# Sigmoid attention and SwiGLU on one core: one eviction moved ahead of the Silu, side work dealt evenly, and the output stage's banks and loads in another order

## The chip, the cores and the metric

The kernel runs on one core of a Trainium2 chip. The metric is device time in microseconds (us), from the first to the last instruction of one execution with what lies around it. Five engines work from queues of their own, each in the order in which its instructions were written: TensorE (PE, matmuls; its weight loads are PEld), VectorE (DVE), ScalarE (ACT), GpSimd (POOL, all but unused here) and SyncE (SP), which issues the DMA transfers.

## The reference, cut to what matters

```python
scores = q @ k.T / 8 - log(448)            # 4 batches, 12 heads, 448 tokens, head dim 64
x = (sigmoid(scores) @ v)                  # -> 1792 tokens x 768
xn = x / sqrt(mean(x * x) + 1e-6) * rms_g
g, val = xn @ w_gate, xn @ w_val           # 768 -> 1536
out = (silu(g) * val) @ w_out              # 1536 -> 768, float32
```

## The kernel before, in words

Every float32 product is made of float16 products: an operand is split into a rounded part ("hi", made by ScalarE) and the rest ("lo", made by VectorE), and three of the four cross products are added up in PSUM (`PARTS`). The weights arrive as 64-bit words and are turned into float32 by three VectorE steps (L430, L431, L432). On top of that both matrix stages of the SwiGLU use a seven-product scheme in place of eight block products, so sums and differences of operands are formed first and the products of several blocks share partial sums.

There are three stages. **Attention** (to about 137 us) computes scores, sigmoid and the product with v, and normalises. The **quads** (137 to 447 us) compute `silu(g) * val`: one quad is one 256-wide chunk `fc` of d_ff (12 of them) for one half `n` of the batches, 24 quads in all. A quad is seven products of nine 448-column matmuls each (1.70 us a product). The result goes to a DRAM scratch tensor `y_d`. The **output stage** (447 us to the end) multiplies by `w_out`, for seven pairs `p` of token tiles, with products of eighteen 384-column matmuls each.

The order within a quad (`quad`, L529) is written by hand. The first product goes into bank `cb`; ScalarE copies it to `y[:, 0]` (L534). A second product is added to the same bank (L540 copies it to `y[:, 1]`), so it has to wait for the copy L534. A third product goes into `cd`. Then `m2` makes product `ca`, VectorE adds `y[:, 0]` into `g_b` (L551) and ScalarE takes its Silu (L552). `m7` adds another product to `cb`, and ScalarE copies that to `c_b` (L556): the copy of the chained tile. All quads but two leave four closures, `c22`, `m4`, `m3` and `ends`, in a list `behind`; the next quad runs them one by one between its own products. `m4` adds a last product to the old quad's `cb` bank, so it may start only when L556 has read that bank; `m4` comes right after the next quad's first product. `ends` writes the quad's result to `y_d`.

At five places of each quad `fill(0)` to `fill(4)` put side work into the VectorE and ScalarE queues: the split of the next chunk's weights (`split_w`), and three of the 48 steps that prepare `w_out` (`split_o`: load a 768 KB chunk, L430, L431, L432, and for each pair of chunks a rounding L616 on ScalarE and a difference L619 on VectorE). `DONE` says which share of the quad's parts has been issued after each fill. In the last two quads, (11, 0) and (11, 1), the fills load and split the first halves of the activations instead (`load_a`, `split_a`, L646 and L647), through three landing buffers `fa`.

In the output stage seven PSUM banks `pss[p]` take first the "even" and then the "odd" product of each pair. Four of them are tiles of their own (`o`), the others are halves of two-bank tiles (`o2`). ScalarE evicts after the even product (L1007) and after the odd one (L757, `out_end`). VectorE's work stands in one list, `line`, which `run_line` deals out by a small clock of costs: four 2304-column sums of `w_out` (L635, each with a ScalarE rounding L628), seven odd splits, four differences `los` (L631), then `split_p(0)`, `split_p(1)` and so on (adds L662, roundings L665, differences L669). `pair_rest(p)` then makes five products per pair.

Of the kernel before, what the change touches and what calls it, by code (L numbers as in the profile page):

```python
# [24 lines left out]
def attention_then_swiglu(  # L25
# [24 lines left out]
    P = 128  # L50
# [6 lines left out]
    NFC = DFF // P  # L57
# [20 lines left out]
    N_NORM = 34  # L78
    LEFT = {(0, 0): (26, 26, 24, 20, 16), (1, 0): (15, 14, 10, 9, 5), (0, 1): (4, 1, 0, 0, 0)}
    EARLIER = {(0, 0): (2, 0, 0, 0, 0), (1, 0): (0, 0, 0, 0, 0), (0, 1): (0, 0, 1, 1, 1)}  # L80
    DONE = (0.15, 0.3, 0.6, 0.9, 1.0)

    bias_s = const.tile([P, 1], F32, name="bias_s")
    ones = const.tile([P, P], F32, name="ones")
# [5 lines left out]
    XW = 7 * NK * S  # L90
    FW = 7 * NK * P
    RW = 2 * DM
    HW = 2 * S
    SL = NK * S
    xc_room = const.tile([P, NQ * XW], F32, name="xc")
    w_room = const.tile([P, 2 * RW + 3 * FW], F32, name="wr")
# [6 lines left out]
    def words(of, at, *shape, dt=F32):  # L103
        n = math.prod(shape) if dt != F16 else math.prod(shape) // 2
        t = of[:, at : at + n]
        if dt != F32:
            t = t.bitcast(dt)
        names = " ".join("abcdef"[: len(shape)])
        sizes = dict(zip("abcdef", shape))
        return t.rearrange(f"p ({names}) -> p {names}", **sizes)  # L110
# [38 lines left out]
    NM = NFC // 2  # L149
    NT = NQ * NTOK  # L150
    NP = NT // 2
# [8 lines left out]
    TW = NM * P  # L160
    a_o = [words(w_room, n * TW, 2, NM, P, dt=F16) for n in range(NP)]
    assert NP * TW <= 2 * RW + FW
    fa = [words(w_room, 2 * RW + FW + n * TW, NM, P) for n in range(3)]
    F_AT = (xc_room, 4 * OW), (room, C_WORDS + 3 * OW)
    f_o = [words(of, a, 5, NM, P) for of, a in F_AT]
    hs_o = [words(of, a + 5 * TW, 2, 5, NM, P, dt=F16) for of, a in F_AT]
# [5 lines left out]
    def bank(name):  # L172
        return ps_m.tile([P, 512], F32, tag="m", name=name)

    def banks(name):
        return ps_s.tile([P, 2, 512], F32, tag="sc", name=name)
# [275 lines left out]
    def run_load():  # L452
        if loads:
            loads.pop(0)[1]()
# [54 lines left out]
    def run_behind():  # L509
        if behind:  # L510
            behind.pop(0)()

    def product(ps, fc, n, a, b, more=False):

        w = win[fc % 2]
        for c in range(NK):
            for m, (l, r) in enumerate(PARTS):
                nc.tensor.matmul(  # L518
                    ps,
                    w[:, l, b, c],  # L520
                    xc[n, a][:, r, c],
                    start=(not more and c == 0 and m == 0),
                    stop=(c == NK - 1 and m == 2),
                    skip_group_check=more,
                )
# [3 lines left out]
    def quad(fc, n, fill, whole=False):  # L529
        y = y_b[len(y_of) % 3]  # L530
        y_of.append((fc, n))
        pb = bank("cb")
        product(pb[:, :S], fc, n, 0, 0)
        nc.scalar.activation(y[:, 0], pb[:, :S], AF.Copy)  # L534
        run_behind()
        fill(0)
        run_behind()

        product(pb[:, :S], fc, n, 4, 5, True)
        nc.scalar.activation(y[:, 1], pb[:, :S], AF.Copy)  # L540
        run_behind()
        fill(1)
        pd = banks("cd")[:, 0]
        product(pd[:, :S], fc, n, 5, 2)
        run_behind()
        fill(2)

        def m2():
            pa = bank("ca")
            product(pa[:, :S], fc, n, 1, 1)  # L550
            tt(g_b, pa[:, :S], y[:, 0], ALU.add)  # L551
            nc.scalar.activation(g_b, g_b, AF.Silu, scale=UNIT)  # L552

        def m7():
            product(pb[:, :S], fc, n, 3, 4, True)
            nc.scalar.activation(c_b, pb[:, :S], AF.Copy)  # L556

        def c22():
            tt(c_b, pd[:, :S], c_b, ALU.add)

        def m4():
            product(pb[:, :S], fc, n, 6, 3, True)
            stt(y[:, 0], pb[:, :S], SH * UNIT, g_b, ALU.mult, ALU.mult)

        def m3():
            product(pd[:, :S], fc, n, 2, 6, True)
            tt(y[:, 1], pd[:, :S], y[:, 1], ALU.add)  # L567
            nc.scalar.activation(y[:, 1], y[:, 1], AF.Silu, scale=UNIT)  # L568

        def ends():  # L570
            stt(y[:, 1], c_b, SH * UNIT, y[:, 1], ALU.mult, ALU.mult)
            i, m = fc % 2, fc // 2
            nc.sync.dma_start(
                y_d[n * NTOK : n * NTOK + NTOK, :, i, m].rearrange("t p x -> p t x"),
                y.rearrange("p j s -> p (j s)").rearrange("p (t x) -> p t x", x=P),
            )

        if whole:
            m7()
            c22()  # L580
            m2()
            fill(3)
            m4()
            m3()
            fill(4)
            behind.extend((wait, wait, ends))
        else:
            m2()
            fill(3)
            m7()  # L590
            fill(4)
            behind.extend((c22, m4, m3, ends))

# [2 lines left out]
    def load_o(c):  # L596
        nc.sync.dma_start(raw_o.rearrange("p f w -> p (f w)"), w_out[c * P : c * P + P, :])
# [42 lines left out]
    def load_a(p, i):  # L640
        nc.sync.dma_start(fa[(p + i * NP) % 3], y_d[2 * p, :, i])

    def split_a(p, i):
        f = fa[(p + i * NP) % 3]
        return [
            lambda: nc.scalar.activation(a_o[p][:, 0], f, AF.Copy),  # L646
            lambda: tt(a_o[p][:, 1], f, a_o[p][:, 0], ALU.subtract),  # L647
        ]
# [31 lines left out]
    line, done, ready = [], set(), set()  # L680
# [110 lines left out]
    def at_once(parts):  # L791
        return [x for x in parts if x[0] is not wait]
# [50 lines left out]
    with tc.manual_schedule():  # L843
# [59 lines left out]
        def fill_norm(where):  # L903
            left = LEFT[where]

            def fill(at):
                run_load()
                while len(later) > left[at]:
                    later.pop(0)[0]()
                for part, *_ in third[: EARLIER[where][at]]:  # L910
                    part()
                del third[: EARLIER[where][at]]

            return fill
# [3 lines left out]
        def fill_steps(*steps):  # L918
            def fill(at):
                for p in steps[at]:  # L920
                    if p == fed[0]:
                        load_a(p, 0)
                        fed[0] += 1
                    else:
                        for part in split_a(p, 0):
                            part()

            return fill

        def fill_with(parts):  # L930
            parts = at_once(parts)
            n = len(parts)

            def fill(at):
                run_load()
                run_load()
                while len(parts) > n - round(n * DONE[at]):
                    parts.pop(0)[0]()

            return fill  # L940
# [4 lines left out]
        for fc, n in order:  # L945
            if (fc, n) in LEFT:
                fill = fill_norm((fc, n))
            elif (fc, n) == (1, 1):
                fill = fill_with(third)
            elif fc + 1 < NFC:  # L950
                if n == 0:
                    split[fc + 1] = split_w(fc + 1)
                parts = at_once(split[fc + 1][n])
                if (fc, n) == (2, 0):
                    outs = split_o()
                    load_o(0)
                    share = -(-len(outs) // (2 * (NFC - 3)))
                new, outs = outs[:share], outs[share:]
                k = len(parts) // max(len(new), 1)
                for i, x in enumerate(new):  # L960
                    parts.insert((i + 1) * k + i, (x, 0.0))
                fill = fill_with(parts)
            elif n == 0:
                assert not outs
                fill = fill_steps([], [0, 1, 2], [], [0, 3], [1, 2, 4, 5])
            else:
                fill = fill_steps([3, 6], [4], [5], [6], [])
            quad(fc, n, fill, (fc, n) in ((1, 1), (NFC - 1, NQ - 1)))


# [2 lines left out]
        pss = [bank("o") for _ in range(4)]  # L973
        for _ in range(2):
            both = banks("o2")
            pss += [both[:, 0], both[:, 1]]
        pss = [pss[x] for x in (0, 1, 3, 4, 5, 2, 6)]
        for p in range(3):
            load_a(p, 1)
        load_p(0)  # L980
# [1 line left out]
        def odd(p):  # L982
            hi, lo = split_a(p, 1)

            def both():
                hi()
                lo()
                if p + 3 < NP:
                    load_a(p + 3, 1)

            return [(None, 0.0, {("even", p)}), (both, 0.95, [("odd", p)])]

        sums, los = sums_o()
        line.extend((x, cost, ()) for x, cost in sums)
        for p in range(NP):
            line.extend(odd(p))
        line.extend((x, cost, ["w"]) for x, cost in los)
        line.append((lambda: load_p(1), 0.0, ()))
        for p in range(NP):
            if p > 1:  # L1000
# [43 lines left out]
```

## Time and profile before

| | |
|---|---|
| median of 3 timed runs | 619.41 us (616.53 to 622.06) |
| the profiled execution | 611.99 us, span 610.2 us |
| TensorE busy, VectorE, ScalarE | 571.0 us (94%), 438.6 (72%), 264.8 (43%) |
| mean granted TensorE clock | 0.985 of full speed |
| TensorE busy from 200 to 440 us (240 us) | 221.5 us |
| TensorE busy from 440 to 500 us (60 us) | 48.9 us |
| TensorE busy from 500 to 560 us (60 us) | 60.0 us |

A row of the timeline gives the start, the length, the engine, the line and operation, the output and inputs, how many instructions were merged, and in brackets how long the engine had been idle and which instruction ended that. A row on waits gives the waiting engine and line, the instruction that it waited for, and the total, the number and the longest. The clock row has one digit for each fortieth of the span (15.3 us).

### The profile page before, as it was taken

Reading aid. Unit: us, or ns where it says so; the run is one execution under the profiler, and the core shown is the slowest. Engines: PE = TensorE matmul, PEld = TensorE weight load, DVE = VectorE, ACT = ScalarE, POOL = GpSimd, SP = SyncE. Lnnn points to the kernel's source line nnn. Section 1 sums busy time; section 2 is a strip of 40 time slices with the busy share of each in tenths; the row PEclk is TensorE's granted clock in tenths of the full one; section 3 lists DMA queues with packets and bytes.
Section 4 is the critical chain, followed back from the end, with each engine's and each line's share of the span. In section 5 each row is a group of like instructions: output and inputs, shape, how many; then the busy total and the mean of one; then the engine's idle time right before and its main releaser. Section 6 shows DMA issues by size and latency. Waiting matters only on the chain.

```text
span 610.2 us, 10226 instructions
## 1 busy us (share of the span) xinstructions
PE 571.0 (94%) x4230; PEld 307.4 (50%) x4230; DVE 438.6 (72%) x576; ACT 264.8 (43%) x397; POOL 0.7 (0%) x6
## 2 busy tenths in 40 slices
PE   8999999999999989898898989899997969999997
PEld 6546554445544544354454445445553536666664
DVE  4697999988769667586876767674584882777761
ACT  5888898875423323323233332423456250222220
POOL 0000000000000000000000000000000000000000
PEclk9999999999999999899999999999997979999999
DMA  8999999830154652727365273612654175155411
GB/s 265 250 221 249 275 273 220 167 61 1 31 152 138 191 136 83 185 74 191 102 180 153 82 186 91 155 32 56 186 178 167 27 253 149 43 154 161 122 39 40
DMA packets 98704, 87.24 MB, mean 143 GB/s; under 512 B 39007, under 2 KB 91746, under 8 KB 98658
## 3 DMA queue, kind: packets, MB, share of 16 engines
q1 hardware_dynamic: 98098, 85.91, 54.2%
q8 instruction: 33, 0.54, 0.4%
q10 hardware_dynamic: 560, 0.69, 0.3%
q14 instruction: 13, 0.11, 0.1%
HBM read 61.34 MB, written 16.52 MB: 128 GB/s over the span
## 4 chain that ended last, share of the span: by engine, by line
PE 65%; DVE 16%; ACT 7%; DMA 5%; issue 5%; SPq 0%; DVEq 0%; ACTq 0%
PE cb L518 17%; PE cd L518 9%; PE av L287 9%; PE oc L707 7%; PE od L707 7%; PE sc L272 6%; PE o L707 4%; PE ob L707 3%; DMA xc<-in_moe_w_out_dram 3%; PE ca L518 2%; DVE wr L431 2%; ACT room L276 2%; DVE wr L432 2%; DVE room L635 2%; DVE xc L631 2%
## 5 line engine op out<-in xcount | busy, mean ns | idle before, releaser
L518 PEld LDWEIGHTS <-wr 128*128 128x128 f16 x1512 | 148.1, 98 | 162.4 <-issue 26.9
L518 PE MATMUL cb<-xc,wr 128*128 128x448 f16 x756 | 151.2, 355 | 18.8 <-ACT room L556 17.9
L276 ACT ACTIVATE room<-sc 128x896 f32<-128x896 f32 x84 | 75.2, 931 | 16.9 <-PE sc L272 16.3
L287 PE MATMUL av<-room 64*64 64x448 f32 x672 | 74.2, 538 | 0.4 <-DMA room<-in_v_dram 0.4
L518 PE MATMUL cd<-xc,wr 128*128 128x448 f16 x324 | 65.2, 353 | 0.0
L272 PE MATMUL sc<-xc 64*64 64x448 f16 x1008 | 59.7, 351 | 2.0 <-ACT room L276 1.1
L707 PE MATMUL o<-room,wr 128*128 128x384 f16 x252 | 45.3, 346 | 11.1 <-ACT room L757 6.6
L567 DVE TENSOR_TENSOR room<-cd,room 128x448 f32<-128x448 f32 x24 | 15.0, 624 | 47.9 <-PE cd L518 47.9
L552 ACT ACTIVATE room<-room 128x448 f32<-128x448 f32 x24 | 13.8, 577 | 81.2 <-DVE room L551 81.2
L272 PEld LDWEIGHTS <-xc 64*64 64x64 f16 x1008 | 32.0, 107 | 32.5 <-issue 21.8
L707 PEld LDWEIGHTS <-xc 128*128 128x128 f16 x360 | 35.2, 98 | 23.3
L518 PE MATMUL ca<-xc,wr 128*128 128x448 f16 x216 | 44.8, 353 | 0.0
L488 DVE SCALAR_TENSOR_TENSOR wr<-wr 128x1536 f16<-128x1536 f32 (+3 forms) x28 | 37.9, 1355 | 8.6 <-ACT wr L485 8.3
L707 PEld LDWEIGHTS <-wr 128*128 128x128 f16 x252 | 25.9, 103 | 30.4 <-issue 15.6
L540 ACT ACTIVATE room<-cb 128x448 f32<-128x448 f32 x24 | 13.0, 542 | 62.1 <-PE cb L518 62.1
L287 PEld LDWEIGHTS av<-room 64*64 64x64 f32 x672 | 27.5, 133 | 23.3 <-issue 16.3
L485 ACT ACTIVATE wr<-wr 128x768 f16<-128x768 f32 (+1 forms) x48 | 35.5, 762 | 0.0
L707 PEld LDWEIGHTS <-room 128*128 128x128 f16 x270 | 26.4, 98 | 17.5
L665 ACT ACTIVATE xc<-xc 128x1536 f16<-128x1536 f32 (+1 forms) x12 | 14.5, 1260 | 46.4 <-DVE xc L662 46.4
L568 ACT ACTIVATE room<-room 128x448 f32<-128x448 f32 x24 | 13.8, 577 | 45.0 <-DVE room L567 45.0
L482 DVE TENSOR_TENSOR wr<-wr 128x384 f32<-128x384 f32 x48 | 26.1, 552 | 0.6
L647 DVE TENSOR_TENSOR wr<-wr 128x768 f16<-128x768 f32 x14 | 13.2, 956 | 17.3 <-ACT wr L646 17.3
(98 smaller groups left out, 676.5 us busy)
## 6 DMA issues: line engine op xcount, KB each, us to landing
y_d<-room SPq DMA_DIRECT2D x24, 448.0 KB, 3.3
xc<-in_moe_w_out_dram SPq DMA_DIRECT2D x12, 768.0 KB, 5.0
room<-in_v_dram SPq DMA_DIRECT2D x24, 224.0 KB, 4.1
wr<-y_d SPq DMA_DIRECT2D x14, 384.0 KB, 3.9
out_dram<-room SPq DMA_DIRECT2D x49, 96.0 KB, 2.2
wr<-in_moe_w_gate_dram SPq DMA_DIRECT2D x12, 384.0 KB, 5.7
wr<-in_moe_w_gate_dram SPq DMA_DIRECT2D x24, 192.0 KB, 6.2
wr<-in_moe_w_val_dram SPq DMA_DIRECT2D x12, 384.0 KB, 6.9
```

Of the source, the lines that this page charges most:

```text
L272: nc.tensor.matmul(o, T[rows, 1, l, c, cols], T[rows, 0, m, :, cols], start=(n == 0), stop=(n == 2))
L276: nc.scalar.activation(a, ps[:, :, :S], AF.Sigmoid, bias=-math.log(S), scale=1.0 / (math.sqrt(D) * SQ * SQ))
L287: nc.tensor.matmul(ps[D * (j ^ r) : D * (j ^ r) + D, :S], v_b[u % 2][rows, r, c], a[rows, r], start=(c == 0), stop=(c == NSLOT - 1),)
L482: first.append((lambda o=o, f0=f0, f1=f1: tt(wf[:, o], wf[:, f0], wf[:, f1], ALU.subtract), 0.6))
L485: nc.scalar.activation(t[:, 0, s], wf[:, s], AF.Copy, scale=SW)
L488: stt(t[:, 1, s], wf[:, s], SW, t[:, 0, s], ALU.mult, ALU.subtract)
L518: nc.tensor.matmul(ps, w[:, l, b, c], xc[n, a][:, r, c], start=(not more and c == 0 and m == 0), stop=(c == NK - 1 and m == 2), skip_group ...
L552: nc.scalar.activation(g_b, g_b, AF.Silu, scale=UNIT)
L567: tt(y[:, 1], pd[:, :S], y[:, 1], ALU.add)
L568: nc.scalar.activation(y[:, 1], y[:, 1], AF.Silu, scale=UNIT)
L665: return lambda: nc.scalar.activation(s[:, 0, a:b], f[:, a:b], AF.Copy), 0.0, ()
L707: nc.tensor.matmul(ps[:, :HALF], a(m, l), w(m, r), start=(not more and m == 0 and n == 0), stop=(m == NM - 1 and n == 2), skip_group_check ...
```

## The change

Six edits. (1) The sum L551 and the Silu become a step of their own, `gate`, which the 22 quads that are not `whole` run after `m7`; so ScalarE's copy to `c_b` stands ahead of the Silu, and `fill(3)` stands ahead of the sum. (2) `DONE` deals the side work in equal fifths. (3) The landing buffers `fa` move from the weights' room to the room that held the raw `w_out` chunk, and the loads and splits of the last two quads stand at other fills. (4) The share of `w_out` steps per quad is worked out with 17 in place of 18: 48 / 18 and 48 / 17 both round up to 3, so nothing moves. (5) The banks of the output pairs change places. (6) The odd splits and the differences `los` of `line` are interleaved.

```diff
-    DONE = (0.15, 0.3, 0.6, 0.9, 1.0)
+    DONE = (0.2, 0.4, 0.6, 0.8, 1.0)
...
-    fa = [words(w_room, 2 * RW + FW + n * TW, NM, P) for n in range(3)]
+    fa = [words(xc_room, XW + 5 * SL + n * TW, NM, P) for n in range(3)]
...
+        pa = bank("ca")
+
         def m2():
-            pa = bank("ca")
             product(pa[:, :S], fc, n, 1, 1)
+
+        def gate():
             tt(g_b, pa[:, :S], y[:, 0], ALU.add)
             nc.scalar.activation(g_b, g_b, AF.Silu, scale=UNIT)
...
             m2()
+            gate()
             fill(3)
             m4()
...
             m2()
             fill(3)
             m7()
+            gate()
             fill(4)
             behind.extend((c22, m4, m3, ends))
...
-                    share = -(-len(outs) // (2 * (NFC - 3)))
+                    share = -(-len(outs) // (2 * (NFC - 3) - 1))
...
-                fill = fill_steps([], [0, 1, 2], [], [0, 3], [1, 2, 4, 5])
+                fill = fill_steps([0, 1, 2], [], [0, 3], [1], [2, 4, 5])
             else:
-                fill = fill_steps([3, 6], [4], [5], [6], [])
+                fill = fill_steps([3, 6], [], [4], [5], [6])
...
-        pss = [pss[x] for x in (0, 1, 3, 4, 5, 2, 6)]
+        pss = [pss[x] for x in (0, 1, 4, 3, 2, 5, 6)]
...
-        for p in range(NP):
-            line.extend(odd(p))
-        line.extend((x, cost, ["w"]) for x, cost in los)
+        for ps_, lo in (((0, 1, 2), los[:1]), ((3, 4), los[1:2]), ((5,), los[2:3]), ((6,), los[3:])):
+            for p in ps_:
+                line.extend(odd(p))
+            line.extend((x, cost, ["w"]) for x, cost in lo)
```

The diff alone doesn't show where the instructions end up. ScalarE's queue from the second half of quad (8, 0) to the middle of (8, 1), before (L552 Silu, L616 rounding of `w_out`, L556 copy to `c_b`, L534 and L540 the next quad's two copies, L568 the second Silu, L485 the weights' rounding):

```order
L568 ACTIVATE room<-room 128x448
L552 ACTIVATE room<-room 128x448
L616 ACTIVATE room<-room 128x3x384
L556 ACTIVATE room<-cb 128x448
L534 ACTIVATE room<-cb 128x448
L485 ACTIVATE wr<-wr 128x768
L540 ACTIVATE room<-cb 128x448
```

and now, with the lines of the changed file (L555 Silu, L559 copy, L571 second Silu, L621 rounding):

```order
L571 ACTIVATE room<-room 128x448
L621 ACTIVATE room<-room 128x3x384
L559 ACTIVATE room<-cb 128x448
L555 ACTIVATE room<-room 128x448
L534 ACTIVATE room<-cb 128x448
L485 ACTIVATE wr<-wr 128x768 x2
L540 ACTIVATE room<-cb 128x448
```

The copy from `cb` and the rounding have passed the Silu; the Silu now stands right in front of the next quad's L534.

VectorE's queue in quad (9, 0), from `m3`'s sum (L567) to the next quad's `c22` (L559); `room<-xc` steps belong to `w_out`, `wr<-wr` steps to the weights, and L551 is the sum that the Silu waits for. Before:

```order
L567 TENSOR_TENSOR room<-cd,room 128x448
L432 SCALAR_TENSOR_TENSOR room<-xc,room 128x2x384
L571 SCALAR_TENSOR_TENSOR room<-room 128x448
L431 SCALAR_TENSOR_TENSOR wr<-wr 128x1536
L432 SCALAR_TENSOR_TENSOR wr<-wr 128x1536
L430 TENSOR_SCALAR room<-xc 128x2x384
L482 TENSOR_TENSOR wr<-wr 128x384
L551 TENSOR_TENSOR room<-ca,room 128x448
L482 TENSOR_TENSOR wr<-wr 128x384
L431 SCALAR_TENSOR_TENSOR room<-xc,room 128x2x384
L482 TENSOR_TENSOR wr<-wr 128x384 x2
```

and now (L570, L574, L554 are the old L567, L571, L551):

```order
L570 TENSOR_TENSOR room<-cd,room 128x448
L432 SCALAR_TENSOR_TENSOR room<-xc,room 128x2x384
L431 SCALAR_TENSOR_TENSOR wr<-wr 128x1536
L574 SCALAR_TENSOR_TENSOR room<-room 128x448
L432 SCALAR_TENSOR_TENSOR wr<-wr 128x1536
L430 TENSOR_SCALAR room<-xc 128x2x384
L482 TENSOR_TENSOR wr<-wr 128x384 x2
L431 SCALAR_TENSOR_TENSOR room<-xc,room 128x2x384
L554 TENSOR_TENSOR room<-ca,room 128x448
L482 TENSOR_TENSOR wr<-wr 128x384 x2
```

One weight step has moved ahead of `ends`; one 384-column subtraction and one step of `w_out` now stand in front of the sum.

ScalarE's queue in the output stage, the last even evictions and all odd ones, with the tiles' numbers (o2_4308 is one two-bank tile). Before (L1007 even, L757 odd evictions, L665 roundings of `split_p`, L646 of the odd splits):

```order
L1007 ACTIVATE room_76<-o2_4308 128x384
L646 ACTIVATE wr_75<-wr_75 128x768 x2
L1007 ACTIVATE room_76<-o2_4308 128x384
...
L757 ACTIVATE room_76<-o_4307 128x384
L665 ACTIVATE xc_74<-xc_74 128x1536 x2
L757 ACTIVATE room_76<-o2_4308 128x384
L665 ACTIVATE xc_74<-xc_74 128x768
L757 ACTIVATE room_76<-o2_4308 128x384
L665 ACTIVATE room_76<-room_76 128x1536
L757 ACTIVATE room_76<-o_4306 128x384
```

and now (L762 odd evictions, L670 roundings):

```order
L762 ACTIVATE room_76<-o2_4308 128x384
L670 ACTIVATE xc_74<-xc_74 128x1536 x2
L762 ACTIVATE room_76<-o_4307 128x384
L670 ACTIVATE xc_74<-xc_74 128x768
L762 ACTIVATE room_76<-o_4306 128x384
L670 ACTIVATE room_76<-room_76 128x1536
L762 ACTIVATE room_76<-o2_4308 128x384
L670 ACTIVATE room_76<-room_76 128x1536
L670 ACTIVATE room_76<-room_76 128x768
L762 ACTIVATE room_76<-o2_4309 128x384
```

The two evictions of o2_4308 belonged to pairs 3 and 4, one right after the other; now they belong to pairs 2 and 5, and the second one stands behind a rounding of `split_p(1)` (`room_76<-room_76`).

## Rows read from the trace of the kernel before

**Rows 1.** The page: granted TensorE clock, in tenths, by fortieths of the span.

```profile
PEclk9999999999999999899999999999997979999999
```

**Rows 2.** Who waited for whom, whole span: total us, times, longest.

```profile
ACT room L552 <- DVE room L551: 81.2, 24, 7.2
...
PE cb L518 <- ACT room L556: 17.9, 9, 2.7
...
ACT room L534 <- PE cb L518: 8.1, 9, 1.1
...
PE o L707 <- ACT room L757: 6.6, 1, 6.6
...
PE o L707 <- ACT room L1007: 4.5, 1, 4.5
```

**Rows 3.** Timeline of PE in the quads: start, length, operation, idle time before it.

```profile
250.66 5.12 PE L518 MATMUL cb<-xc,wr 128*128 128x448 f16 x18 [2.73 <-ACT room L556]
...
304.66 3.56 PE L518 MATMUL cb<-xc,wr 128*128 128x448 f16 x18 [1.55 <-ACT room L556]
330.60 3.56 PE L518 MATMUL cb<-xc,wr 128*128 128x448 f16 x18 [1.94 <-ACT room L556]
...
358.02 3.57 PE L518 MATMUL cb<-xc,wr 128*128 128x448 f16 x18 [2.73 <-ACT room L556]
384.71 3.57 PE L518 MATMUL cb<-xc,wr 128*128 128x448 f16 x18 [2.69 <-ACT room L556]
```

**Rows 4.** Timeline of DVE and ACT at the end of quad (9, 0).

```profile
382.05 0.56 DVE L430 TENSOR_SCALAR room<-xc 128x768 uint32<-128x768 uint32 x1 [1.33 <-DMA xc<-in_moe_w_out_dram]
...
383.00 0.62 DVE L551 TENSOR_TENSOR room<-ca,room 128x448 f32<-128x448 f32 x1
383.53 0.55 DVE L482 TENSOR_TENSOR wr<-wr 128x384 f32<-128x384 f32 x1
383.65 0.58 ACT L552 ACTIVATE room<-room 128x448 f32<-128x448 f32 x1 [7.17 <-DVE room L551]
384.00 0.95 DVE L431 SCALAR_TENSOR_TENSOR room<-xc,room 128x768 uint32<-128x768 uint32 x1
...
384.55 0.54 ACT L534 ACTIVATE room<-cb 128x448 f32<-128x448 f32 x1
```

**Rows 5.** Timeline of DVE and ACT at the end of quad (8, 0).

```profile
353.92 0.95 DVE L432 SCALAR_TENSOR_TENSOR room<-xc,room 128x768 uint32<-128x768 uint32 x1
...
355.26 0.61 DVE L551 TENSOR_TENSOR room<-ca,room 128x448 f32<-128x448 f32 x1
...
356.39 1.15 ACT L616 ACTIVATE room<-room 128x1152 f16<-128x1152 f32 x1
```

**Rows 6.** Timeline of DVE in quad (7, 0): the result's last step and its wait.

```profile
323.15 0.62 DVE L571 SCALAR_TENSOR_TENSOR room<-room 128x448 f32<-128x448 f32 x1 [0.64 <-ACT room L568]
```

**Rows 7.** Timeline of PE in the output stage.

```profile
447.32 11.86 PE L707 MATMUL o<-room,wr 128*128 128x384 f16 x72
463.71 23.16 PE L707 MATMUL o<-room,wr 128*128 128x384 f16 x126 [4.53 <-ACT room L1007]
493.47 10.26 PE L707 MATMUL o<-room,wr 128*128 128x384 f16 x54 [6.60 <-ACT room L757]
503.56 3.09 PE L707 MATMUL ob<-xc 128*128 128x384 f16 x18
```

**Rows 8.** Timeline of DVE in the output stage.

```profile
449.33 10.33 DVE L635 TENSOR_TENSOR room<-room 128x2304 f32<-128x2304 f32 x4
462.58 2.80 DVE L647 TENSOR_TENSOR wr<-wr 128x768 f16<-128x768 f32 x3 [2.92 <-ACT wr L646]
...
477.34 9.96 DVE L631 SCALAR_TENSOR_TENSOR xc<-room,xc 128x2304 f16<-128x2304 f32 x4
487.21 3.93 DVE L662 TENSOR_TENSOR xc<-xc 128x768 f32<-128x768 f32 x4
491.70 4.30 DVE L669 TENSOR_TENSOR xc<-xc 128x1536 f16<-128x1536 f32 x3 [0.56 <-ACT xc L665]
```

## The prediction

> **What bounds the kernel now.** I read the granted clock first, then who waited for whom, then the timeline of TensorE at each wait, and last the queues of the engine that it waited for. The clock is full but for three places, in the 17th, the 31st and the 33rd fortieth [rows 1]. TensorE is busy for 94% of the span, so what can be won is its idle time and its time at the lower clock level. Its named idle time is of two kinds [rows 2]. Nine times, 17.9 us together, it waits in the quads for L556, ScalarE's copy of the chained tile. Twice, 4.5 and 6.6 us, it waits in the output stage for an eviction. ScalarE itself isn't short of time: its Silu stood idle for 81.2 us in all behind VectorE's sum L551. Instructions leave ScalarE in order, so all that stands behind the Silu waits with it, the copy too. The timeline shows where: after the quads (3, 0) to (10, 0), and these pauses repeat four chunks later (1.94, 2.73 and 2.69 after (7, 0), (8, 0) and (9, 0), the same within 0.05 after (3, 0) to (5, 0), 1.55 after (6, 0)) [rows 3]. One of the 2.73 us pauses was followed by eighteen matmuls in 5.12 us, where the others took 3.56 [rows 3]: 1.2 in place of 2.4 GHz for part of them, 1.56 us lost. The two pauses of the output stage did the same: 126 matmuls in 23.16 us and 54 in 10.26 [rows 7], where 72 at full clock took 11.86, or (11.86 - 0.33) / 71 = 0.162 us each, the last one's own 0.33 set aside. That makes 20.6 and 8.9, so 2.55 and 1.34 were lost. The three together: 5.45 us.
>
> **The copy ahead of the Silu, and the even dealing.** They go together, since both move VectorE's sum. Without the Silu in front, the copy runs when its product ends, and `m4` can start at once. But the wait is handed on: the next product on the new `cb` bank needs L534, and L534 still stands behind the Silu. `m4` gives 1.70 us of cover, which is what one product lasts.
>
> Take quad (9, 0) [rows 3, 4]. TensorE was free at 384.71 - 2.69 = 382.02. Before, the sum started at 383.00, the Silu at 383.65, the copy behind it, and TensorE at 384.71. Now `m4` runs from 382.02 to 383.72. The sum comes later: ahead of it stand one more subtraction (0.47, from 383.53 to 384.00) and one step of `w_out` (0.87 start to start), 1.34 together. So it starts at 384.34, ends at 384.96, the Silu at 385.5 lets L534 go, which ends at 386.05. TensorE waits 2.3 us instead of 2.69. The step L430 that waits for a transfer until 382.05 holds this sum in either order, so the earlier dealing helps nothing here. The gain is a mere 0.4.
>
> Quad (8, 0) is of another sort [rows 3, 5]. TensorE was free at 355.29. The rounding L616 (1.15 us) can begin when L432 ends at 354.87 and ends at 356.0; the copy ends at 356.5, which leaves a pause of 1.2 instead of 2.73. The sum moves from 355.26 to 355.73, L534 ends at 357.4, and `m4` lasts to 358.2: no second pause.
>
> In general, the new pause is the old one less 1.74 (the cover of 1.70, and 0.04 by which the order on ScalarE gets shorter), plus what the sum is late. After (6, 0) the sum is late by 0.47 + 0.87: 1.55 - 1.74 + 1.34 = 1.15. After (7, 0) it is late by 0.47 + 0.47, but a weight step now fills the 0.64 us in which VectorE stood idle ahead of L571 [rows 6]: 1.94 - 1.74 + 0.94 - 0.64 = 0.5. Quad (10, 0) has no `w_out` steps; its sum comes sooner and I leave nothing. Sum left: 2 x 0.5 + 2 x 1.2 + 2 x 2.3 + 1.15 = 9.15. The ninth wait (17.9 less the eight, 0.75) is in the first quads, where the copy, the table that the first Silu loads and L534 come in a new order; I leave 0.75 there, between 0 and 2. **Saved: 17.9 - 9.15 - 0.75 = 8.0 us.** Bounds: 17.9, if the even dealing gets every sum out in time, and 0, if each pause merely changes its instruction.
>
> **The landing buffers, and the loads of the last two quads.** TensorE shows no idle time between the last of the eight pauses and 459.18 (463.71 - 4.53) [rows 7], and the loads are issued a fill sooner than before, so these cost nothing; their cover is the products between the fills. A late load would hold ScalarE's L646, behind it L556 and L534, and so a product: one pause of 0.5 to 2.7 [rows 3]. One thing is dearer: the last split now stands in front of the last `ends`, and VectorE starts the sums of `w_out` later by one difference (2.80 / 3 = 0.93 [rows 8]) and some of the rounding in front of it, say 1.2 us. The share of `w_out` steps is 3 before and after: nothing.
>
> **The banks of the output pairs.** Both long pauses lie between pairs 3 and 4, the two halves of one two-bank tile. The pause of 4.53 ends with pair 3's even eviction and that of 6.60 with its odd one [rows 7], and ScalarE had both behind work that waits for VectorE. Now pairs 2 and 5 share the tile, two products apart, so both pauses go. Here a rule speaks against this reading. The Trainium skill (PSUM — Partial Sum Buffer, "PSUM bank collisions raise a hardware error") has engines kept apart by bank and quadrant, and says that accesses on different banks "run clean". By that rule a matmul into one half wouldn't have to wait for an eviction of the other, the two pauses would have another cause, and the sum would lack this gain. In the trace TensorE did resume after just that eviction, both times; what makes it wait is then the program, which tracks the tile and not the bank. I go by the rows, and keep the rule as a rival.
>
> Without pauses the fourteen products take 14 x 2.92 = 40.9 us, from 447.32 to 488.2 instead of 503.56 [rows 7]. What is late next is VectorE. Its first odd difference moves from 462.58 to about 463.8. From there it has seven odd differences (7 x 0.93 = 6.5), four `los` (9.96), the four adds of `split_p(0)` (3.93), a wait of 0.56 and three differences (4.30), and three adds of `split_p(1)` (3/4 of 3.93) [rows 8]: 28.2 us, to 492.0. Interleaving changes their order, not this sum. ScalarE then makes a rounding (491.70 - 490.16 = 1.5 us, third add to first difference [rows 8]) and only behind it the odd eviction of pair 5 (about 0.5): 494.0. The second product of `pair_rest(0)` takes that tile and could start at 488.2 + 2.92 = 491.1. **So a new pause of 2.9 us stands there; saved: 4.53 + 6.60 - 2.9 = 8.2.** Bounds for it: 0, and 6.6, the longest pause of this stage.
>
> **The clock.** Three drops cost 5.45. After the change, pauses of 2.3 and less stay in the quads, none of which size dropped the clock before, and one of 2.9, between 2.73 (dropped once in two rows) and 4.53 (dropped). I take one drop at the smallest price seen, 1.6; bounds 0 and 2 x 2.55. **Saved: 3.85.**
>
> **Sum:** 8.0 + 8.2 + 3.85 = 20.1 us. The profiled execution took 612.0, so its like would take 591.9. The timed runs lie 4.5 to 10 above the profiled one, for which the trace has no reason; I take the saving off their median: 619.4 - 20.1 = **599.3**.
>
> **The rivals.**
> 1. The pauses in the quads merely change hands: the sum is late enough that each L534 waits as long as L556 did. For it: rows 4, where that happens. Against: rows 5. Then 599.3 + 8.0 = 607.3. Chance 0.11.
> 2. The output stage pauses as long as now in its new place, 6.6 us, with the clock's 2.55: 599.3 + 3.7 + 0.95 = 604.0. For it: VectorE's list has no slack. Against: it moves by only 1.2. Chance 0.09.
> 3. VectorE gets ahead: no pause in `pair_rest(0)`, no drop, and half of the 9.15 gone: 599.3 - 2.9 - 1.6 - 4.6 = 590.2. Chance 0.07.
> 4. The bank order isn't what makes TensorE wait, as the rule would have it; both pauses stay with their drops: 599.3 + 8.2 + (2.55 + 1.34 - 1.6) = 609.8. Chance 0.04.
> 5. Slower: `gate` behind `fill(3)` makes the sum late in all 22 quads, also where it now has room. It decides once the sum ends more than 0.65 us after TensorE is free (1.70 less 0.5 for the Silu and 0.54 for L534); each microsecond beyond that costs 22, and 1.2 would give 599.3 + 26.4 = 625.7. Against: in nine quads ScalarE stood waiting for the product with L534 (8.1 us [rows 2]), so the sum is early there. Chance 0.02.
>
> The forecast has 0.67, with a range of its own of 595 to 604. To 592 and 608 the range takes in rivals 1 and 2 and part of 3. About 1%, 6 us, is what can be told from no change: faster than 613.2 are the forecast and rivals 1 to 4, less a tail, 0.94; slower than 625.6 half of rival 5 and what I overlook, 0.015; the rest within 1%, 0.045.
>
> **What would show it.** TensorE's waits for the copy fall from 17.9 to about 3, and waits for the next quad's L534 appear, some 6 to 7 us in all, the longest, 2.3, after (5, 0) and (9, 0). No pause between pairs 3 and 4; `pair_rest(0)` starts about 41 us after the first output product, and its second product waits 2 to 4 us for an odd eviction. VectorE's sums of `w_out` start about 3 us after the first output product, 2.0 before. Waits for L534 in quads with n = 1 would prove me wrong, or a pause between the even products.

## The result, and the profile after

The changed kernel takes 595.1 us (median of 4 runs, 592.0 to 598.3), the kernel before 618.0 (4 runs, 613.8 to 622.1): a ratio of 0.963, 95% interval 0.955 to 0.972. That is 22.8 us less; 20.1 were forecast. The medians in the table of experiments leave out an execution more than 1.5% above the fastest of its kernel as slow: one of e7's two, and one of the nine of the kernel before that ran beside e1 to e4.

The profiled executions differ by less, 612.0 and 598.3 us, and the stages say why. A stage's length is read from TensorE's timeline: attention to the last sums of squares (L340), the quads from there to the first product of the output stage, and the output stage to the end of the span.

| us | attention | quads | output | span |
|---|---|---|---|---|
| before | 137.6 | 309.7 | 162.9 | 610.2 |
| changed | 142.0 | 300.4 | 154.1 | 596.5 |

Attention, which no edit touches, took 4.4 us longer in the profiled run of the changed kernel. Most of that is TensorE's wait for the loads of v, 4.1 us there and 0.4 before (the first 143 us, before and then changed):

```profile
PE av L287 <- DMA room<-in_v_dram: 0.4, 1, 0.4
PE av L287 <- DMA room<-in_v_dram: 4.1, 2, 3.1
```

In the profiles below attention takes 136.2 to 140.7, whatever the kernel. So the stages are compared from here on, each as one profiled execution shows it: the quads lost 9.3 us and the output stage 8.8.

TensorE's waits from 130 to 520 us of the changed kernel (waiting engine and line, what ended the wait, total, times, longest), to set beside [rows 2]:

```profile
PE cb L518 <- ACT room L534: 8.7, 8, 2.7
PE od L712 <- ACT room L762: 3.6, 1, 3.6
PE cb L518 <- ACT room L559: 2.3, 2, 1.1
PE cd L518 <- DVE room L562: 1.1, 2, 0.8
```

The 17.9 us of waits for the copy (now L559) have become 2.3, and the waits for the next quad's L534 have grown from 0.6 to 8.7 us. The two pauses of the output stage are gone, and one of 3.6 has come. The timeline of TensorE in the quads shows each of them [rows 3]:

```profile
154.84 1.86 PE L518 MATMUL cb<-xc,wr 128*128 128x448 f16 x9 [1.10 <-ACT room L534]
179.96 1.86 PE L518 MATMUL cb<-xc,wr 128*128 128x448 f16 x9 [0.84 <-ACT room L534]
...
229.46 1.86 PE L518 MATMUL cb<-xc,wr 128*128 128x448 f16 x9 [0.45 <-ACT room L534]
...
253.83 3.57 PE L518 MATMUL cb<-xc,wr 128*128 128x448 f16 x18 [1.14 <-ACT room L559]
282.23 1.86 PE L518 MATMUL cb<-xc,wr 128*128 128x448 f16 x9 [2.71 <-ACT room L534]
307.14 1.86 PE L518 MATMUL cb<-xc,wr 128*128 128x448 f16 x9 [0.92 <-ACT room L534]
331.58 1.86 PE L518 MATMUL cb<-xc,wr 128*128 128x448 f16 x9 [0.45 <-ACT room L534]
...
355.47 3.56 PE L518 MATMUL cb<-xc,wr 128*128 128x448 f16 x18 [1.14 <-ACT room L559]
382.78 1.86 PE L518 MATMUL cb<-xc,wr 128*128 128x448 f16 x9 [1.61 <-ACT room L534]
```

A row of nine matmuls after a wait for L534 is the product that continues the new `cb` bank; a row of eighteen after L559 is `m4`. The pauses after (3, 0) to (9, 0) stand in order from 229.46 on; after (10, 0) there is none. The output stage, TensorE's timeline [rows 7]:

```profile
442.37 41.11 PE L712 MATMUL o<-room,wr 128*128 128x384 f16 x252
483.32 3.09 PE L712 MATMUL ob<-xc 128*128 128x384 f16 x18
490.01 5.90 PE L712 MATMUL od<-xc 128*128 128x384 f16 x18 [3.61 <-ACT room L762]
```

All fourteen products run in one piece, 41.0 us. The second product of `pair_rest(0)` waits 3.61 us and then takes 5.90 us where the one before took 3.09: 2.81 us lost at the lower clock level. The page's clock row shows it as the only drop:

```profile
PEclk9999999999999999999999999999999988999999
```

VectorE in that stage [rows 8]:

```profile
445.98 10.33 DVE L640 TENSOR_TENSOR room<-room 128x2304 f32<-128x2304 f32 x4
459.23 2.80 DVE L652 TENSOR_TENSOR wr<-xc,wr 128x768 f16<-128x768 f32 x3 [2.92 <-ACT wr L651]
...
485.08 3.93 DVE L667 TENSOR_TENSOR room<-room 128x768 f32<-128x768 f32 x4
489.62 4.38 DVE L674 TENSOR_TENSOR room<-room 128x1536 f16<-128x1536 f32 x3 [0.61 <-ACT room L670]
```

The sums start 3.6 us after the first output product (before: 2.0), and the adds of `split_p(1)`, behind whose rounding the awaited eviction stands, run until 489.0.

### The profile page after: what moved, and what is told of

Same layout as the page of the kernel before. It is cut to its first block, busy times and chain, and to the rows that moved or that the text cites. A ratio compares the mean times of both kernels' runs of the same rounds, so it can differ in the third digit from the quotient of the medians.

```text
span 596.5 us, 10249 instructions
## 1 busy us (share of the span) xinstructions
PE 567.8 (95%) x4230; PEld 307.1 (51%) x4230; DVE 437.1 (73%) x576; ACT 265.9 (45%) x397; POOL 0.7 (0%) x6
## 4 chain that ended last, share of the span: by engine, by line
PE 62%; DVE 17%; DMA 8%; ACT 6%; issue 4%; SPq 2%; DVEq 0%; ACTq 0%
PE cb L518 18%; PE cd L518 11%; PE od L712 7%; PE oc L712 7%; PE av L287 5%; PE ca L518 4%; PE sc L272 4%; PE o L712 3%; PE ob L712 3%; DMA xc<-in_moe_w_out_dram 2%; DMA xc<-in_k_dram 2%; DVE wr L432 2%; DVE wr L431 2%; ACT room L276 1%; SPq L189 1%
## 5 line engine op out<-in xcount | busy, mean ns | idle before, releaser
L518 PE MATMUL cb<-xc,wr 128*128 128x448 f16 x756 | 149.4, 352 | 11.4 <-ACT room L534 8.7
L570 DVE TENSOR_TENSOR room<-cd,room 128x448 f32<-128x448 f32 x24 | 15.0, 625 | 53.9 <-PE cd L518 53.9
L712 PE MATMUL o<-room,wr 128*128 128x384 f16 x252 | 41.1, 326 | 0.0
L559 ACT ACTIVATE room<-cb 128x448 f32<-128x448 f32 x24 | 13.0, 542 | 56.8 <-PE cb L518 37.5
L670 ACT ACTIVATE xc<-xc 128x1536 f16<-128x1536 f32 (+1 forms) x12 | 14.5, 1260 | 45.8 <-DVE xc L667 45.8
L485 ACT ACTIVATE wr<-wr 128x768 f16<-128x768 f32 (+1 forms) x48 | 34.8, 760 | 0.0
L571 ACT ACTIVATE room<-room 128x448 f32<-128x448 f32 x24 | 13.9, 577 | 45.6 <-DVE room L570 45.6
L540 ACT ACTIVATE room<-cb 128x448 f32<-128x448 f32 x24 | 13.1, 544 | 46.1 <-PE cb L518 46.1
L712 PE MATMUL od<-xc 128*128 128x384 f16 x144 | 27.5, 350 | 3.6 <-ACT room L762 3.6
```

The costliest lines, as they stand in the source:

```text
L485: nc.scalar.activation(t[:, 0, s], wf[:, s], AF.Copy, scale=SW)
L518: nc.tensor.matmul(ps, w[:, l, b, c], xc[n, a][:, r, c], start=(not more and c == 0 and m == 0), stop=(c == NK - 1 and m == 2), skip_group ...
L670: return lambda: nc.scalar.activation(s[:, 0, a:b], f[:, a:b], AF.Copy), 0.0, ()
L712: nc.tensor.matmul(ps[:, :HALF], a(m, l), w(m, r), start=(not more and m == 0 and n == 0), stop=(m == NM - 1 and n == 2), skip_group_check ...
```

## The experiments

The stages of all runs, from one profile each, and the medians of their timed runs:

| run | quads | output | median | kernel before, same chip |
|---|---|---|---|---|
| e1 banks only | 308.1 | 156.4 | 606.3 | 616.8 |
| e2 gate only | 308.3 | 163.5 | 610.3 | 616.8 |
| e3 deal only | 306.3 | 164.1 | 612.2 | 616.8 |
| e4 gate and deal | 299.4 | 163.1 | 603.4 | 616.8 |
| e5 line undone | 300.2 | 156.4 | 597.6 | 616.6 |
| e6 landing undone | 299.1 | 151.7 | 591.2 | 616.6 |
| e7 banks undone | 299.6 | 158.2 | 596.0 | 616.6 |
| e8 sum first | 294.1 | 153.0 | 585.1 | 616.6 |
| e9 changed, again | 301.2 | 154.0 | 590.5 | 614.1 |
| e10 sums early | 301.2 | 147.6 | 587.9 | 614.1 |
| e11 both | 294.8 | 147.6 | 584.6 | 614.1 |
| e12 both, dealt sooner | 291.0 | 147.6 | 581.0 | 614.1 |

**e1, the banks alone**, in the kernel before:

```diff
-        pss = [pss[x] for x in (0, 1, 3, 4, 5, 2, 6)]
+        pss = [pss[x] for x in (0, 1, 4, 3, 2, 5, 6)]
```

> Only the order of the seven output banks is changed; all else as before. Theory (the tile is what makes TensorE wait): no pause between pairs 3 and 4 any more; the quads stay at about 310 us; the output stage, 162.9 us before, loses the 11.1 us of pauses, but VectorE's list in its old order (odd splits, then all four differences of w_out) now lies open: pauses of about 1.5 and 1.5 ahead of the odd products and pair_rest and about 4.6 at its second product, some 7 us in all, so the stage comes to 156 to 159. Rival (another cause than the shared tile, as the rule on banks has it): both pauses, 4.5 and 6.6, stay, 163.

Both pauses went and the stage fell by 6.5 us, as the theory had it. The rival is refuted. What came instead, TensorE's waits:

```profile
PE od L707 <- ACT room L757: 4.6, 1, 4.6
...
PE ob L707 <- DVE xc L669: 1.1, 1, 1.1
```

Its quads are those of the kernel before, instruction for instruction, with the same waits, and yet took 1.6 us less (308.1 and 309.7). The clock makes the difference: the pause of 2.73 us that cost 1.56 us at the lower level in the kernel before [rows 3] cost none here.

```profile
250.34 3.56 PE L518 MATMUL cb<-xc,wr 128*128 128x448 f16 x18 [2.73 <-ACT room L556]
```

So a difference of 1.6 us between the quads of two profiles can come from the clock alone.

**e2, the gate alone; e3, the dealing alone; e4, the two together**, in the kernel before:

```diff
@@ e2, e4 (and m2 split into m2 and gate, as in the change)
...
             m2()
             fill(3)
             m7()
+            gate()
             fill(4)
...
@@ e3, e4
-    DONE = (0.15, 0.3, 0.6, 0.9, 1.0)
+    DONE = (0.2, 0.4, 0.6, 0.8, 1.0)
```

> Only the gate is moved behind m7 (copy ahead of the Silu); side work dealt as before, 30% of it in fill(3), which now stands ahead of the sum. Theory (the wait is handed on to L534 unless the sum comes in time): TensorE's waits for the copy fall from 17.9 to under 3, but waits for L534 of 12 to 15 us come in their place; the quads take 305 to 308 us instead of 309.7. Rival (the order on ScalarE alone frees TensorE): the quads take 293 to 297. The output stage stays at 163.

> Only DONE is changed to equal fifths; the Silu stays ahead of the copy. Theory: the sum gets out earlier in the quads with n = 0, the waits for the copy fall from 17.9 to about 14; the quads take 305 to 307 us. Rival (the deal is worth nothing by itself): 309.7. The output stage stays at 163.

> Gate and equal dealing together, nothing of the output stage. Theory: the two need each other; the quads take 299 to 302 us, as in the changed kernel (300.4), more than the sum of the two alone gives back. Rival (they add up): 302 to 305, or what the two single runs make. The output stage stays at 163 with its two pauses.

The gate alone gave the quads 1.4 us. TensorE's waits there (e2) were

```profile
PE cb L518 <- ACT room L534: 14.5, 9, 3.3
...
PE cb L518 <- ACT room L559: 2.5, 2, 1.3
```

17.0 us, of which 0.6 was there before; so 16.4 of the 17.9 us of waits for the copy came back, and nearly the whole wait was handed on. Two of its pauses dropped the clock, where one did before, which hides another 1.6 us of gain:

```profile
278.41 3.35 PE L518 MATMUL cb<-xc,wr 128*128 128x448 f16 x9 [3.32 <-ACT room L534]
...
383.94 3.49 PE L518 MATMUL cb<-xc,wr 128*128 128x448 f16 x9 [3.02 <-ACT room L534]
```

The dealing alone gave 3.4 us, with one drop as before. Together they gave 10.3, with no drop. The waits of e3, and then of e4:

```profile
PE cb L518 <- ACT room L556: 13.8, 8, 2.7
PE cb L518 <- ACT room L534: 8.1, 8, 2.2
...
PE cb L518 <- ACT room L559: 2.3, 2, 1.1
```

By the waits alone, with the 0.6 left out each time, the gate saved 1.5 us, the dealing 4.1 and the two together 8.1, which is 2.5 more than the 5.6 that the single ones add up to. The stage lengths, 10.3 against 4.8, show twice the sum, but most of that excess is the clock. So the two help each other, as the theory has it, by less than the stages suggest. The timed medians don't decide it: 6.5 and 4.6 us alone and 13.3 together, with two executions each of e2 and e4. The theory's reason fits the rows: with the gate the copy no longer waits for the sum, but L534 does, with 1.70 us of cover from `m4`, and only a sum that also comes sooner fits into that cover.

**e5, VectorE's list in its old order**, in the changed kernel:

```diff
-        for ps_, lo in (((0, 1, 2), los[:1]), ((3, 4), los[1:2]), ((5,), los[2:3]), ((6,), los[3:])):
-            for p in ps_:
-                line.extend(odd(p))
-            line.extend((x, cost, ["w"]) for x, cost in lo)
+        for p in range(NP):
+            line.extend(odd(p))
+        line.extend((x, cost, ["w"]) for x, cost in los)
```

> The changed kernel with VectorE's list in its old order: all seven odd splits, then the four differences of w_out. The prediction said that the interleaving moves VectorE's work but doesn't shorten it, and put the new pause down to the sum of that work: then the output stage stays at 154, with one pause of 3.6 us. Rival: in the old order VectorE stands idle while it waits for odd splits whose loads haven't landed or whose even products haven't ended, so its list ends later: pauses ahead of pair_rest and at its second product, 8 to 9 us in all, stage 159 to 162. The second single-part run points to the rival. The quads stay at 300.

The stage took 156.4, 2.3 more than with the interleaving: my step in the prediction was wrong, and the rival too large. VectorE's timeline (the odd differences L652, then the four of `w_out`, L636) shows the idle time that the interleaving fills:

```profile
459.81 0.96 DVE L652 TENSOR_TENSOR wr<-xc,wr 128x768 f16<-128x768 f32 x1 [2.36 <-ACT wr L651]
461.46 0.96 DVE L652 TENSOR_TENSOR wr<-xc,wr 128x768 f16<-128x768 f32 x1 [0.69 <-ACT wr L651]
462.57 0.96 DVE L652 TENSOR_TENSOR wr<-xc,wr 128x768 f16<-128x768 f32 x1 [0.15 <-ACT wr L651]
464.79 0.96 DVE L652 TENSOR_TENSOR wr<-xc,wr 128x768 f16<-128x768 f32 x1 [1.26 <-ACT wr L651]
465.66 9.96 DVE L636 SCALAR_TENSOR_TENSOR xc<-room,xc 128x2304 f16<-128x2304 f32 x4
```

4.46 us of waits for ScalarE's roundings; in the changed kernel such a wait between the first odd difference and the last is 0.99 in all. TensorE then pauses three times, 5.45 us together, where the changed kernel has one pause of 3.61:

```profile
480.05 0.50 PE L712 MATMUL ob<-xc 128*128 128x384 f16 x2 [1.14 <-ACT xc L670]
481.84 4.31 PE L712 MATMUL ob<-xc 128*128 128x384 f16 x16 [1.29 <-DVE xc L674]
489.17 4.38 PE L712 MATMUL od<-xc 128*128 128x384 f16 x18 [3.02 <-ACT room L762]
```

**e6, the landing buffers, loads and splits of the last two quads as before:**

```diff
-    fa = [words(xc_room, XW + 5 * SL + n * TW, NM, P) for n in range(3)]
+    fa = [words(w_room, 2 * RW + FW + n * TW, NM, P) for n in range(3)]
...
-                fill = fill_steps([0, 1, 2], [], [0, 3], [1], [2, 4, 5])
+                fill = fill_steps([], [0, 1, 2], [], [0, 3], [1, 2, 4, 5])
...
-                fill = fill_steps([3, 6], [], [4], [5], [6])
+                fill = fill_steps([3, 6], [4], [5], [6], [])
```

> The changed kernel with the landing buffers, loads and splits of the last two quads as before. Theory: the last split no longer stands ahead of ends, VectorE starts its sums 1.2 us sooner after the first output product (2.0 to 2.4 us, not 3.6), and the pause at the second product of pair_rest(0) falls from 3.6 to about 2; if that is too short to drop the clock, the stage falls from 154.1 to 150 or 151, else to 152.5. Rival (moving them cost nothing): 154, pause 3.6. The quads stay at 300.

The stage fell to 151.7, between the theory's values with and without a clock drop: the pause shrank to 2.2, but the clock still dropped.

```profile
483.89 4.76 PE L712 MATMUL od<-xc 128*128 128x384 f16 x18 [2.20 <-ACT room L762]
```

VectorE's sums started at 439.66, 2.0 us after the first output product at 437.65. So the changed kernel is better off without this edit, by 2.5 us of this stage in these two profiles. The pause has 1.4 of it; the other 1.1 is the smaller loss at the lower clock level (1.67 against 2.81), which also differs after pauses of one length, as the last section shows.

**e7, the banks in the old order**, in the changed kernel (the edit of e1 reversed).

> The changed kernel with the old order of the output banks. Theory: with pairs 3 and 4 in one tile again, TensorE waits for pair 3's evictions: one pause of about 6.3 us between the odd products; the even one is short or gone where the eviction comes in time, another of about 2 later; stage 159 to 163. Rival (the interleaved list alone removes the pauses): 154 or less. The quads stay at 300.

```profile
454.01 22.68 PE L712 MATMUL o<-room,wr 128*128 128x384 f16 x126 [6.13 <-ACT room L1013]
478.80 8.94 PE L712 MATMUL o<-room,wr 128*128 128x384 f16 x54 [2.11 <-ACT room L762]
```

Both pauses are back, and the stage is 158.2, just under the 159 to 163 expected. I had them the wrong way round: the long one is at the even eviction (L1013), 1.6 us longer than before, which is what the sums in front of it start later, and the short one at the odd.

**e8, the sum right behind its product**, only the Silu behind the copy, in the changed kernel:

```diff
         def gate():
-            tt(g_b, pa[:, :S], y[:, 0], ALU.add)
             nc.scalar.activation(g_b, g_b, AF.Silu, scale=UNIT)
...
             m2()
+            tt(g_b, pa[:, :S], y[:, 0], ALU.add)
             fill(3)
             m7()
             gate()
```

> The changed kernel, but VectorE's sum stays right behind its product, ahead of fill(3), and only ScalarE's Silu goes behind the copy. If the waits for L534 that are left come from the sum standing behind fill(3), they shrink by what stood in front of it (0.5 to 1.3 us each): after (5, 0) and (9, 0) from 2.7 and 1.6 to 0.5 to 1.3, and the quads take 295 to 298 us instead of 300.4. Rival (they come from VectorE being late altogether, or from the transfers of w_out): 300. The output stage stays at 154 with its pause.

The quads fell to 294.1, and the waits for L534 from 8.7 to 2.4 us:

```profile
PE cb L518 <- ACT room L534: 2.4, 4, 1.1
```

The difference was the price of moving the sum together with the Silu.

**e9, the changed kernel again, and e10, the sums of `w_out` early:** in e10 each of the quads (10, 0) to (11, 1) issues one of the four sums at its `fill(0)`, and `line` begins with their roundings.

```diff
+        sums, los = sums_o()
+        tts = [x for x, _ in sums[0::2]]
+        def early(fill):                      # wraps the fill of the last four quads
+            def both(at):
+                fill(at)
+                if at == 0:
+                    tts.pop(0)()
+            return both
...
-        sums, los = sums_o()
-        line.extend((x, cost, ()) for x, cost in sums)
+        line.extend((x, 2.45, ()) for x, _ in sums[1::2])
```

> The changed kernel once more, beside the next three on one chip. 592 to 598 us; quads about 300, output stage 154.

> The changed kernel, but VectorE's four 2304-column sums of w_out are issued in quads (10, 0) to (11, 1), one at fill(0) of each, where VectorE otherwise waits for TensorE; their roundings stay where they were. Theory (VectorE's list, 10.3 us of it the sums, sets the pause at the second product of pair_rest(0)): the list starts some 7 us sooner, the pause and its clock drop go, the output stage takes 147 to 149 us instead of 154, the quads 300 to 301. Rival (the eviction waits for something else, such as the reload of an odd half): a pause of 2 us or more stays, 151 or more; or the sums cost as much in the quads as they save, quads 304 or more.

The pause and its clock drop are gone, the stage is 147.6, and the quads are what they are in e9, run on the same chip (301.2 both):

```profile
441.32 41.11 PE L712 MATMUL o<-room,wr 128*128 128x384 f16 x252
482.27 3.09 PE L712 MATMUL ob<-xc 128*128 128x384 f16 x18
485.19 3.09 PE L712 MATMUL od<-xc 128*128 128x384 f16 x18
```

The medians, 587.9 and 590.5, differ by 2.6 only, less than the 6.4 between the stages. The profiled execution of e9 is the slowest of its four, 597.7 us at a mean granted clock of 0.990; the other three took 588.9 to 591.9 at 0.997 to 1.000. So of the 6.4 the clock drop, 2.8, is not lost in every execution; the pause of 3.4 is what the sums cost.

**e11, e8 and e10 together; e12, the same with `DONE = (0.25, 0.5, 0.7, 0.85, 1.0)`.**

> The sum right behind its product (as in the run that gave quads of 294) and the sums of w_out early, together: quads 294 to 296, output stage 147 to 149, 577 to 581 us; they touch different pauses, so they should add up.

> As the run with both, and the side work dealt sooner still: shares of 0.25, 0.5, 0.7, 0.85 and 1. If what is left in the quads (about 6.5 us: copies behind a rounding that waits for VectorE, c22 behind a transfer, a few L534) comes from VectorE steps issued too late in a quad, it falls by 3 to 5 us: quads 290 to 292, 573 to 577 us. Rival (steps dealt sooner get in the way of m3's and ends' sums, or hold ScalarE's copies): 294 or more. Output stage 147 to 149.

The stages came as expected (294.8 and 147.6, 291.0 and 147.6). The times that I gave for the whole were about 6 us too low. e11's profiled execution, with an attention of 136.2, took 580.4, inside the 577 to 581 given, but its other three took 584.4 to 586.5; e12's attention took 140.1, and nothing on record has the stages of the others. TensorE's waits in e12:

```profile
PE cb L518 <- ACT room L534: 1.7, 2, 1.1
PE cb L518 <- DVE wr L488: 1.0, 1, 1.0
PE cd L518 <- DVE room L564: 0.8, 2, 0.4
```

e12 has the lowest median: 581.0 us, 0.947 of the kernel before (0.941 to 0.953). That it beats e11 (0.952, 0.945 to 0.958) is read from the quads, for the intervals overlap. The changed kernel, on the same chip, is at 0.964 (0.956 to 0.973).

## Why the prediction was right, and where it was not

**The copies.** The mechanism held to the instruction: copy free, `m4` at once, then a wait for L534 where the sum is late. The pauses forecast and found: after (3, 0) and (7, 0) 0.5, found 0.45 both; after (4, 0) and (8, 0) 1.2, found 1.14 both, and for the copy, behind the rounding, as said; after (6, 0) 1.15, found 0.92; after (10, 0) none, none. After (5, 0) and (9, 0) 2.3, found 2.71 and 1.61. In e9 the first of these was 2.33, so it moves from run to run; the step that holds the sum there, L430, waited 1.70 us for a transfer in the first profile and 1.33 in e9's. In the first quads I left 0.75 and found 1.10 + 0.84 + 0.63 = 2.57, the third a wait of that size that the kernel before had too, about 190 us in. So the waits fell from 18.5 (17.9 and that 0.6) to 11.0, by 7.5, where 8.0 were forecast; with the 1.56 of the clock that makes 9.1 of the quads' 9.3. One sign was misworded: each wait forecast stands behind a quad with n = 0 and so in the next one, whose n is 1. Meant were waits behind a quad with n = 1, and the only one is that 0.63. e2 to e4 show the cause: neither edit does it alone, for the waits fall by 1.5 and 4.1 with one of them and by 8.1 with both. The forecast costed the two together and so never said how little the gate is worth by itself.

**The banks.** Shown by e1 and e7, from both sides. The rule of the Trainium skill (PSUM — Partial Sum Buffer, "PSUM bank collisions raise a hardware error"), that accesses on different banks run clean, isn't contradicted. In all four rows, two before and two in e7, the wait ends with the eviction of the tile's other half; I read this as the program keeping its dependencies by the two-bank tile, and no run separates that from another reason by which the two halves are tied. By the rule alone one would have missed 6.5 us of the stage in e1.

**The new pause.** Forecast 2.9 at the second product of `pair_rest(0)`, found 3.6 there (3.4 in e9), for the eviction that was named, behind the rounding that was named. That VectorE's list sets it is shown by e10: with 10.3 us of sums out of the list the pause is gone. The two old pauses and the new one together gave 7.5, not 8.2. Two terms were mis-sized. The sums started 1.6 us later against the first output product, not 1.2. And the clock drop cost 2.81, not 1.6, so the clock gave back 2.6 of its 5.45, not 3.85.

**The step that failed** is the sentence that interleaving changes the order of VectorE's work, not its sum. The work is the same, but in the old order VectorE waits for roundings between the odd differences; e5 puts that at 2.3 us of the stage, 1.8 of them in TensorE's pauses. The forecast wasn't hurt by it, since it counted the waits of the new order as nearly nothing.

**The landing buffers** were costed at 1.2 us through the later sums; e6 shows 2.5, 1.4 of pause and 1.1 of clock. Their edit is the one part that works against the rest.

**Why 22.8 and not 20.1?** The two stages together gained 9.3 + 8.8 = 18.1 us in the profiled pair, and the three terms, 8.0, 8.2 and 3.85, came out at 7.5, 7.5 and 2.6. So the forecast was 2 us too high by its own terms, and the medians came out higher for a reason that it doesn't have: that 22.8 lies so near 20.1 is in part luck. Of the 4.7 us between 18.1 and 22.8 the record shows where some may lie. In the 18 executions of the kernel before that the medians beside the experiments are made of, the time goes with the mean granted clock: 610.5 to 614.0 us at 0.988, 611.4 to 614.1 at 0.985, 616.6 to 619.4 at 0.978, 618.7 to 618.8 at 0.975. The profiled one, 612.0 at 0.985, is a quick one, and the kernel's median of 618.0 is what 0.978 goes with. So the usual execution seems to lose more to the clock than the profile from which the forecast was made, and the reason that the prediction missed for the 4.5 to 10 us between them may lie there. The clocks of the four timed executions behind 618.0 are not on record, so how much of the 4.7 this makes stays open.

## What to carry to other kernels

When an instruction is moved ahead of one that waits, look at what now stands right behind the wait: in e2 16.4 us of 17.9 came back, because the wait went to the next copy on the same queue. Split such a step where the wait is: the sum early and the Silu late (e8) was worth another 6 us of the quads. And where the tail of a stage is set by one engine's list, start the parts of it that need nothing from that stage earlier, in the waits of the stage before (e10). Before stages are compared, look at the granted clock after each pause in both profiles: e1's quads were 1.6 us shorter than before with no edit in them.

## What the runs showed of the hardware

Whether a pause drops TensorE's clock was not to be told from its length alone. A pause of 2.71 us in the changed kernel's quads was followed by nine matmuls in 1.86 us, at full clock; one of 2.33 at the same place in e9 by nine in 3.52, and one of 2.13 there in e10 by nine in 3.22:

```profile
280.18 3.52 PE L518 MATMUL cb<-xc,wr 128*128 128x448 f16 x9 [2.33 <-ACT room L534]
279.42 3.22 PE L518 MATMUL cb<-xc,wr 128*128 128x448 f16 x9 [2.13 <-ACT room L534]
```

In the output stage a pause of 2.20 (e6) and one of 3.54 (e8) were both followed by eighteen matmuls in 4.76 us, and one of 3.61 by 5.90, against 3.09 at full clock. So pauses of 2 to 4 us cost 0 to 2.8 us on top of themselves; I had taken 1.6 for one and nothing for those of 2.3 and less.

```profile
479.40 4.76 PE L716 MATMUL od<-xc 128*128 128x384 f16 x18 [3.54 <-ACT room L766]
```
